# Two value banks by turns, an earlier norm of q and another order of first loads in the first phase of an attention and feed-forward kernel

## The chip, the cores and the metric

The kernel runs on one core of a Trainium2 chip. The metric is the device time of one execution in microseconds (us); for several runs the median is given. The profile names the engines PE (TensorE's matmuls), PEld (its weight loads), DVE (VectorE), ACT (ScalarE), POOL (GpSimd) and SP (SyncE, which issues most DMAs here). Each engine works through its own queue in order and waits at an instruction until what that one needs is there.

## The reference

The reference computes attention with RMS-normalized queries and keys for 8 batches, 12 heads, 448 positions and a head size of 64, and then a feed-forward block with a squared ReLU on the 3584 tokens:

```python
def rmsnorm(x, g):
    rms = np.sqrt(np.mean(x * x, axis=-1, keepdims=True) + 1e-06)
    return x / rms * g
q_n, k_n = (rmsnorm(q, g_q), rmsnorm(k, g_k))
scores = scale * np.matmul(q_n, k_n.transpose(0, 1, 3, 2))
scores = scores - np.max(scores, axis=-1, keepdims=True)
attn = np.exp(scores)
attn = attn / (np.sum(attn, axis=-1, keepdims=True) + 1e-09)
x = np.matmul(attn, v)                  # (B, H, S, D), then laid out as (B*S, H*D)
h = np.maximum(x @ w_in, 0.0)           # 768 -> 2048
out = h * h @ w_out                     # 2048 -> 768
```

All inputs and outputs are float32.

## The kernel before

**Pairs.** Two heads of one batch are worked on together as a pair, so there are 48 pairs, numbered through by batch and head. The 448 positions are three blocks of 128 and a rest of 64; the rests of an even pair and the odd pair behind it share one block. The function `alone(i)` is true for the first twelve pairs (batches 0 and 1). They are worked on with no feed-forward beside them: this is the first phase. From then on attention of later pairs is woven into the feed-forward of earlier ones.

**One pair.** The rows of q and k are squared (`square`, L179 on ACT or L181 on POOL), summed and turned into mean squares (`add`, L192 and L195 on DVE) and raised to the power -1/2 (`power`, L201 on POOL, for q and k in one instruction through its arguments `first` and `number`). Then q alone is scaled by it (`scale`, L216 on POOL); k's factor is applied later, as the scale of the exponential (L392). `turn` transposes k and q on PE (L357, L360), k into PSUM bank 7 and q into bank 6. ACT copies kT (L367), DVE copies qT and multiplies it by the gains (L365). `weigh` makes the scores into banks 0 to 3 (L387) and their exponentials on ACT (L392); as the keys lie on the partitions, this is the weight matrix already turned. `attend` multiplies the weights by the values into bank 4 (L455), `add_weights` sums them up with a matrix of ones into bank 5 (L468). `take_sums` transposes the sums by blocks on DVE (L496); `invert` makes the reciprocals in all columns (four small copies L505, then L506, L511, L512); `finish` multiplies bank 4 by them (L524) and so makes xT, the input of the feed-forward. Behind some `finish` calls `begin_forms` makes differences of xT for a fast matrix product (L548, on DVE and POOL).

**Visits.** In the first phase each pair i has two visits, n = 0 and n = 1, of `visit_alone`. Visit 0 loads v of pair i, makes two key blocks of the scores of pair i, transposes k and q of pair i+1, squares q (ACT) and k (POOL) of pair i+2, calls `begin(step)`, and attends three key blocks of pair i-1 with their first two sums. Visit 1 normalizes pair i+2 (`normalize`: both adds on DVE, one power for both, q's scaling), makes the other scores of pair i, calls `begin(step)`, issues the loads of q and k of pair i+4 and attends the last key block of pair i-1, with its last sums, `take_sums`, `invert` and `finish`. Each visit ends with `begin(step + 1)`. `step` is 4i + 2n, so four steps go to a pair.

**Weights for the feed-forward.** In between, `begin` brings the weights into another form, a piece at a time: it makes up to two pending sums of pieces (`make_sum`, L884, by turns on DVE and POOL) and, when the step has reached the next due time in the list `early`, calls `convert`. That joins the piece split before (three DVE operations, L838, L858, L862), loads the words of the piece after the next (SP, L806 or L811, three buffers) and splits one piece (three ACT operations, L825 to L827). The list `early` holds 17 times, 2.4 steps apart, beginning with step 0.

**The start.** The kernel loads the two gain rows (ACT's queue), q and k of pair 0 and of pair 1. `load_full` loads the three whole blocks of a pair's q or k with two DMAs (L157), `load_rest` the rests of two pairs with two more (L166). On ACT an exponential of one number (L83) makes it load its table; its output goes to `g_most`, which DVE overwrites with the greatest gain (L87). If that is small enough (L90, `bounded`), the program runs without a subtraction of the maximum; this is the branch that runs here. `normalize_first` prepares pairs 0 and 1, with q scaled on DVE.

**Later phases.** `visit_among` and `put_in_order` do the same work in the midst of the products, through lists of tasks. `put_in_order` calls `rescale` for a pair, hence one power and one scaling. These pairs attend into bank 4 and sum into bank 3; q's and k's transposes go through bank 0 or through DRAM. Banks 7, 6 and 5 are then the accumulators of the products (`roles`, L596).

Of the kernel before, what the change touches and what calls it, by code (L numbers as in the profile page):

```python
# [13 lines left out]
F32 = mybir.dt.float32  # L14
I32 = mybir.dt.int32
U32 = mybir.dt.uint32
AF = mybir.ActivationFunctionType
ALU = mybir.AluOpType
# [18 lines left out]
@with_exitstack  # L37
def kernel(
    ctx: ExitStack,
    tc: tile.TileContext,  # L40
    q: bass.AP,
    k: bass.AP,
    v: bass.AP,
    g_q: bass.AP,
    g_k: bass.AP,
    moe_w_in: bass.AP,
    moe_w_out: bass.AP,
    out: bass.AP,
):

    nc = tc.nc
    D = q.shape[3]
    const = ctx.enter_context(tc.tile_pool(name="const", bufs=1))
    wide = const.tile([P, P + D], F32, name="wide")
    ident = wide[:, 0:P]  # L60
    ones = const.tile([P, D], F32, name="ones")
    minus_half = const.tile([P, 1], F32, name="minus_half")
    g = const.tile([P, 1], F32, name="g")
    g_most = const.tile([1, 1], F32, name="g_most")
    bounded = const.tile([1, 1], I32, name="bounded")
    rows = Rows(nc, SimpleNamespace(io=const, small=const), q, k, ones, minus_half)
    with (
        tc.tile_pool(name="early", bufs=1) as early,
        tc.tile_pool(name="gains", bufs=1, space=bass.MemoryType.PSUM) as psum,
        tc.manual_schedule(engines=ENGINES),  # L70
    ):
        g_rows = early.tile([1, 2, D], F32, name="g_rows")
        for n, row in enumerate((g_q, g_k)):
            nc.scalar.dma_start(g_rows[:, n], row.rearrange("(one d) -> one d", one=1))
        rows.load_full(0, 0, nc.sync)
        rows.load_full(0, 1, nc.scalar)
        for x in range(2):
            rows.load_rest(0, x, nc.sync)
        for x in range(2):
            rows.load_full(1, x, nc.sync)  # L80
        nc.vector.memset(ones, 1.0)
        nc.vector.memset(minus_half, -0.5)
        nc.scalar.activation(g_most, ones[0:1, 0:1], AF.Exp)  # L83
        make_identity(nc, ident)
        nc.gpsimd.tensor_copy(out=wide[:, P : P + D], in_=ident[:, 0:D])
        nc.vector.tensor_tensor(out=g_rows[:, 0], in0=g_rows[:, 0], in1=g_rows[:, 1], op=ALU.mult)
        nc.vector.tensor_reduce(  # L87
            out=g_most, in_=g_rows[:, 0], axis=AX.X, op=ALU.max, apply_absolute_value=True
        )
        nc.vector.tensor_scalar(  # L90
            out=bounded, in0=g_most, scalar1=MOST_G, scalar2=None, op0=ALU.is_le
        )
        gains = psum.tile([P, 1], F32, name="gains")
        for e in range(2):
            nc.tensor.matmul(
                gains[ds(e * D, D), :], lhsT=g_rows[:, 0], rhs=ones[0:1, 0:1], start=True, stop=True
            )
        for x in range(2):
            rows.normalize_first(0, x, early.tile([P, 2 * P + 2 * P], F32, name=f"squares{x}"))
        nc.scalar.mul(g, gains, D**-0.5)  # L100
    flag = nc.values_load(bounded, min_val=0, max_val=1)
    with tc.If(flag > 0) as either:
        program(tc, rows, v, g, wide, moe_w_in, moe_w_out, out, shift=False)
    with either.Else():
        program(tc, rows, v, g, wide, moe_w_in, moe_w_out, out, shift=True)

class Rows:

# [1 line left out]

    def __init__(self, nc, pools, q, k, ones, minus_half):
        self.nc, self.pools, self.qk = nc, pools, (q, k)
        self.ones, self.minus_half = ones, minus_half
        self.B, self.H, self.S, self.D = q.shape
        self.rooms = [
            pools.io.tile([P, 2, NG, 2, self.D], F32, name=f"qk{n}", tag=f"qk{n}") for n in range(2)
        ]
        self.squares, self.ms, self.rr = {}, {}, {}  # L120
        self.in_blocks = lambda i: False
# [74 lines left out]
            out=ms, in0=ms, scalar1=1.0 / self.D, scalar2=1e-6, op0=ALU.mult, op1=ALU.add  # L196
        )

    def power(self, i, first, number):
        ms = self.ms[i][:, first : first + number, 0 : self.count(i)]  # L200
        self.nc.gpsimd.tensor_tensor(  # L201
            out=self.rr[i][:, first : first + number, 0 : self.count(i)], in0=ms,
            in1=self.minus_half[:, :, None].to_broadcast(list(ms.shape)), op=ALU.pow,
        )

    def normalize_first(self, i, x, room):

        self.square(i, x, room)
        self.add(i, x)
        self.power(i, x, 1)  # L210
        if x == 0:
            self.scale(i, x, self.nc.vector)

# [6 lines left out]


@with_exitstack
def program(ctx, tc, rows, v, g, wide, moe_w_in, moe_w_out, out, shift):

    nc = tc.nc

# [18 lines left out]
    dram = ctx.enter_context(tc.tile_pool(name="forms", bufs=1, space=bass.MemoryType.DRAM))  # L245

    rows = rows.go_on(io, small, lambda i: in_blocks(i))
    ones = rows.ones
    ident = wide[:, 0:P]
    lasts = [const.tile([P, 2, D], F32, name=f"lasts{n}") for n in range(2)]  # L250
    ones_of = [const.tile([P, SIDE], F32, name=f"ones_of{n}") for n in range(2)]
# [31 lines left out]
    def alone(i):  # L283

        return pairs[i][0] < 2
# [58 lines left out]
            v[b, 2 * c : 2 * c + 2, NJ * P : S].rearrange("h p d -> p h d"),  # L344
        )

    def rescale(i):
        rows.power(i, 0, 2)
        for x in range(2 if shift else 1):
            rows.scale(i, x, nc.gpsimd)  # L350

    def turn(i, x):
# [87 lines left out]
                nc.vector.tensor_copy(out=tiles[NJ][e][mine, part], in_=tr[mine, NJ, :size])  # L440

    def sums_bank(i):
        return banks[5 if alone(i) else 3][:, 0:S]

    def attend(i, some):

        order = values_of(i)  # L450
        for n in some:
            m = order[n]
            mine = ds(i % 2 * LASTS, LASTS) if m == NJ and shift else ds(0, P)
            for e in range(2):
                nc.tensor.matmul(  # L455
                    banks[4][ds(e * D, D), 0:S],
                    lhsT=lasts[i % 2][mine, e, :] if m == NJ else values[i][:, m, e, :],
                    rhs=weights[key_of(i, m), e][mine], start=n == 0, stop=n == NJ,
                )
# [60 lines left out]
    def finish(i):  # L520

        b, c = pairs[i]
        xts[b, c] = new_x()
        nc.vector.tensor_tensor(  # L524
            out=xts[b, c], in0=banks[4][:, 0:S], in1=inverse.pop(i), op=ALU.mult
        )
        for x in range(2):
            del turned[i, x]
        del values[i]
        if b == 1:  # L530
            begin_forms(c)
        elif b % 2 and c >= NK:
            complete.append((b // 2, c - NK))
# [369 lines left out]

    block, tile_pieces = COST // NBLK, 4
    ahead = 4 * tile_pieces
    early = deque(2.4 * n for n in range(ahead + 1))
    every = block / ahead
    late = deque(
        block + 2 + every * (n - 2 * tile_pieces) for n in range(len(all_pieces) - ahead)
# [44 lines left out]
    def begin(step):  # L954
        for _ in range(2):
            make_sum()
        while early and early[0] <= step:
            early.popleft()
            convert()
            end_join()  # L960
# [9 lines left out]
        if i <= last:  # L970
            rows.square(i, x, room[:, 0 : 4 * P], engine)

    def normalize(i):

        if i <= last:
            for x in range(2):
                rows.add(i, x)
            rescale(i)

    def weigh_slots(i, n):  # L980
        if not shift:
            for m in slots_of(i, n):
                weigh(i, m)
        elif n:
            weigh_shifted(i)
# [10 lines left out]
    def visit_alone(i, n):  # L996
        step = i * 2 * VISITS + 2 * n
        if n == 0:
            load_v(i)
            if i and shift:  # L1000
                attend_all(i - 1)
            weigh_slots(i, n)
            turn(i + 1, 1)
            turn(i + 1, 0)
            square(i + 2, 0, new_acc())
            square(i + 2, 1, new_acc(), nc.gpsimd)
            begin(step)
            if i and not shift:
                attend(i - 1, range(NJ))
                add_weights(i - 1, (0, 1))  # L1010
                forget(i - 1, (0, 1))
        else:
            normalize(i + 2)
            weigh_slots(i, n)
            begin(step)
            if in_blocks(i + 2):
                store_q(i + 2)
                load_blocks(i + 2, 0)
                load_blocks(i + 2, 1)
            load_qk(i + 4)  # L1020
            if i and not shift:
                attend(i - 1, (NJ,))
                add_weights(i - 1, (2, 3))
                forget(i - 1, (2, 3))
                take_sums(i - 1)
                invert(i - 1)
                finish(i - 1)
            if not alone(i) and not shift:
                additions(i)
        begin(step + 1)  # L1030

    def put_in_order(i):
        rescale(i)
        if in_blocks(i):
            steps = [lambda: store_q(i), lambda: load_blocks(i, 0)]
            for step in steps:
                tasks.extend((lambda: None, lambda: None, step))
# [100 lines left out]
```

## Time and profile before

| | |
|---|---|
| median of three runs | 1462.53 us (1461.55 to 1462.66) |
| the profiled execution | 1461.41 us |
| its span, first to last instruction | 1459.6 us |
| mean granted TensorE clock | 0.998 |
| PE busy in the first 20 us | 10.0 us |
| PE busy from 20 to 140 us | 107.4 of 120 us |
| DVE busy from 20 to 140 us | 92.4 of 120 us |
| first product of the feed-forward (L643) begins | 147.31 us |

Times inside the profile count from the span's start. A line of the timeline gives the start, the duration, the engine, the source line, the operation, what it writes and reads, how many instructions were merged, and in brackets how long the engine had been idle and what ended that. A line of the waits gives the engine and line that waited, what it waited for, the sum in us, how many times, and the longest. Matmuls are pipelined and each float32 matmul is recorded as two instructions; the duration of a merged row reaches from its first start to its last end.

### The profile page before, as it was taken

How to read it: one execution, taken by the hardware profiler on the slowest of the kernel's cores; microseconds unless marked ns; L12 is line 12 of the kernel's file. 1: busy time of each engine (PE TensorE's matmuls, PEld its weight loads, DVE VectorE, ACT ScalarE, POOL GpSimd, SP SyncE). 2: the span in 40 equal slices, each digit the busy share in tenths (PEclk: the TensorE clock that was granted, in tenths of full speed). 3: DMA queues.
4: the chain of work that ended last, by engine and by line, in shares of the span. 5: the costliest groups of instructions: out<-in, count | busy, mean ns of one | idle time of the engine just before them, and what ended most of it. 6: DMA issues, size and time to landing. Idle time of an engine off the chain costs nothing.

```text
span 1459.6 us, 15299 instructions
## 1 busy us (share of the span) xinstructions
PE 1425.6 (98%) x4932; PEld 680.2 (47%) x4932; DVE 667.3 (46%) x1269; ACT 583.7 (40%) x1102; POOL 623.2 (43%) x522
## 2 busy tenths in 40 slices
PE   6989999999999999999999999999999999999998
PEld 2323444444444444445454544445444455555554
DVE  5877356786777623324342542324334251132313
ACT  6764455747555144432514234342332403222130
POOL 4545745655555635353543545245342422021111
PEclk9999999999999999999999999999999999999999
DMA  6565336565667554444435454334523223223122
GB/s 149 164 203 137 76 85 179 168 189 165 197 175 218 160 169 103 137 113 132 118 65 165 117 183 128 109 96 99 169 64 111 82 103 135 87 76 124 38 87 79
DMA packets 309278, 188.11 MB, mean 129 GB/s; under 512 B 265796, under 2 KB 293316, under 8 KB 300996
## 3 DMA queue, kind: packets, MB, share of 16 engines
q1 hardware_dynamic: 308384, 186.84, 43.7%
q8 instruction: 41, 0.67, 0.2%
q14 instruction: 49, 0.40, 0.1%
q10 hardware_dynamic: 804, 0.20, 0.1%
HBM read 144.57 MB, written 42.40 MB: 128 GB/s over the span
## 4 chain that ended last, share of the span: by engine, by line
PE 90%; DVE 4%; issue 3%; POOL 2%; ACT 1%; DMA 1%; SPq 0%; POOLq 0%; DVEq 0%; ACTq 0%
PE bank L643 35%; PE bank L724 29%; PE bank L455 9%; PE bank L387 8%; PE bank L695 5%; PE bank L485 2%; PE bank L468 1%; POOL rr L201 1%; DMA qk<-in_q_dram 1%; DVE few L505 1%; POOL qk L216 0%; DVE inverse L512 0%; DVE out_sb L884 0%; DVE xT L524 0%; DVE acc L765 0%
## 5 line engine op out<-in xcount | busy, mean ns | idle before, releaser
L643 PE MATMUL bank<-xT,in_sb 128*128 128x448 f32 x1344 | 517.5, 542 | 0.0
L643 PEld LDWEIGHTS bank<-xT,in_sb 128*128 128x128 f32 x1344 | 251.7, 190 | 262.4 <-issue 251.1
L765 DVE TENSOR_TENSOR acc<-acc,bank 128x384 f32<-128x384 f32 x324 | 173.7, 549 | 278.8 <-PE bank L724 205.6
L392 ACT ACTIVATE wT<-bank,rr 128x448 f32<-128x448 f32 x288 | 161.1, 631 | 269.1 <-PE bank L387 249.1
L201 POOL TENSOR_TENSOR rr<-ms,minus_half 128x16 f32<-128x16 f32 (+3 forms) x50 | 125.7, 2514 | 333.1 <-DVE ms L195 299.1
L724 PE MATMUL bank<-out_sb,hid 128*128 128x384 f32 x768 | 267.6, 488 | 0.0
L663 DVE TENSOR_TENSOR hid<-bank,part 128x448 f32<-128x448 f32 x128 | 77.0, 622 | 305.3 <-PE bank L643 305.2
L724 PE MATMUL bank<-out_sb,sums 128*128 128x384 f32 x576 | 204.0, 490 | 3.1 <-DVE acc L765 3.0
L724 PEld LDWEIGHTS bank<-out_sb,hid 128*128 128x128 f32 x768 | 144.8, 190 | 107.2 <-issue 6.8
L411 POOL TENSOR_TENSOR sum<-sum,wT 128x448 f32<-128x448 f32 (+1 forms) x144 | 164.3, 1164 | 12.8 <-ACT wT L392 10.4
L387 PE MATMUL bank<-qT,kT 64*128 64x448 f32 (+1 forms) x768 | 164.0, 573 | 3.7 <-ACT qT L330 1.6
L679 POOL TENSOR_TENSOR sums<-hid 128x384 f32<-128x384 f32 x32 | 32.4, 1012 | 291.1 <-ACT hid L665 290.6
L664 ACT ACTIVATE hid<-hid 128x448 f32<-128x448 f32 x128 | 73.3, 572 | 201.0 <-DVE hid L663 200.9
L724 PEld LDWEIGHTS bank<-out_sb,sums 128*128 128x128 f32 x576 | 107.7, 190 | 87.7 <-DVE acc L765 8.2
L650 ACT COPY part<-bank 128x448 f32<-128x448 f32 x128 | 67.7, 529 | 180.5 <-PE bank L643 180.4
L455 PE MATMUL bank<-wT,vt 128*64 128x448 f32 x480 | 106.2, 546 | 0.0
L387 PEld LDWEIGHTS bank<-qT,kT 64*128 64x128 f32 (+1 forms) x768 | 55.2, 173 | 108.9 <-issue 90.8
L411 POOL TENSOR_TENSOR sum<-wT 128x448 f32<-128x448 f32 x72 | 84.1, 1188 | 45.8 <-PE bank L485 45.8
L192 DVE TENSOR_REDUCE ms<-squares 128x8 f32<-128x512 f32 (+1 forms) x68 | 41.9, 617 | 125.6 <-ACT squares L179 125.6
L695 PE MATMUL bank<-out_sb,hid 128*128 128x384 f32 x256 | 86.4, 491 | 0.0
L665 ACT ACTIVATE hid<-hid 128x448 f32<-128x448 f32 x128 | 73.8, 577 | 4.0
L695 PEld LDWEIGHTS bank<-out_sb,hid 128*128 128x128 f32 x256 | 47.6, 190 | 39.3 <-issue 5.7
(83 smaller groups left out, 1126.9 us busy)
## 6 DMA issues: line engine op xcount, KB each, us to landing
out_sb<-out_forms SPq DMA_DIRECT2D x24, 1536.0 KB, 7.4
in_sb<-in_forms SPq DMA_DIRECT2D x24, 1344.0 KB, 5.9
words<-in_moe_w_in_dram SPq DMA_DIRECT2D x32, 384.0 KB, 3.6
words<-in_moe_w_out_dram SPq DMA_DIRECT2D x32, 384.0 KB, 3.6
out_forms<-out_sb SPq DMA_DIRECT2D x8, 1536.0 KB, 6.3
in_forms<-in_sb SPq DMA_DIRECT2D x8, 1344.0 KB, 5.5
qk<-in_q_dram SPq DMA_DIRECT2D x96, 96.0 KB, 3.0
vt<-in_v_dram SPq DMA_DIRECT2D x96, 96.0 KB, 3.3
```

What stands on the lines that cost most here:

```text
L201: self.nc.gpsimd.tensor_tensor(out=self.rr[i][:, first : first + number, 0 : self.count(i)], in0=ms, in1=self.minus_half[:, :, None].to_br ...
L387: nc.tensor.matmul(sc[some], lhsT=turned[p, 1][r, keys], rhs=turned[p, 0][r, :], start=True, stop=True,)
L392: nc.scalar.activation(new_weights((i, m), e), sc, AF.Exp, scale=rows.rr[i][:, 1, 2 * m + e : 2 * m + e + 1],)
L411: nc.gpsimd.tensor_tensor(out=sums[i, e][some], in0=left[some], in1=weights[key_of(i, m), e][some], op=ALU.add)
L455: nc.tensor.matmul(banks[4][ds(e * D, D), 0:S], lhsT=lasts[i % 2][mine, e, :] if m == NJ else values[i][:, m, e, :], rhs=weights[key_of(i, ...
L643: nc.tensor.matmul(ps, lhsT=w_sb[:, IN.index(left), c, :], rhs=forms[u, c][right], start=first and c == 0, stop=c == NK - 1, skip_group_ch ...
L663: nc.vector.tensor_tensor(out=dst, in0=left, in1=right, op=op)
L664: nc.scalar.activation(dst, dst, AF.Relu)
L665: nc.scalar.activation(dst, dst, AF.Square)
L695: nc.tensor.matmul(ps, lhsT=flat[a][:, t, ds(NT * P, P)], rhs=w_sb[t][:, 2 * a + half, :], start=(a, t) == parts[0], stop=(a, t) == parts[-1],
L724: nc.tensor.matmul(ps, lhsT=lefts[left][:, t, ts(tt, P)], rhs=w_sb[t][:, OUT.index(right), :], start=first and t == 0, stop=t == 1, skip_g ...
L765: nc.vector.tensor_tensor(out=acc, in0=acc, in1=ps, op=ALU.add)
```

## The change

- The values of pair i are weighed into bank 4 or bank 5 by turns (`values_bank`), where it was always bank 4. The sums move from bank 5 to bank 6.
- `power` and `rescale` now take one of q and k. In the first phase q's add, power and scaling move from the start of visit 1 to visit 0, behind its first `begin(step)` and ahead of `attend`. k's add and power stay in visit 1, now behind the scores.
- In the later phases `put_in_order` calls the two rescalings one after the other: q's power, q's scaling, k's power.
- The due times in `early` are two steps later each.
- The first loads: q's rest goes through ACT's queue; k's full blocks go through SP's queue, ahead of k's rest.
- The exponential that loads ACT's table writes a tile of its own.
- `ones` is passed to `program` directly, without a change in what is done.

```diff
-        rows.load_full(0, 1, nc.scalar)
-        for x in range(2):
-            rows.load_rest(0, x, nc.sync)
+        rows.load_rest(0, 0, nc.scalar)
+        rows.load_full(0, 1, nc.sync)
+        rows.load_rest(0, 1, nc.sync)
...
-        nc.scalar.activation(g_most, ones[0:1, 0:1], AF.Exp)
+        nc.scalar.activation(early.tile([1, 1], F32, name="some"), ones[0:1, 0:1], AF.Exp)
...
-    def power(self, i, first, number):
-        ms = self.ms[i][:, first : first + number, 0 : self.count(i)]
+    def power(self, i, x):
+
+        ms = self.ms[i][:, x, 0 : self.count(i)]
         self.nc.gpsimd.tensor_tensor(
-            out=self.rr[i][:, first : first + number, 0 : self.count(i)], in0=ms,
-            in1=self.minus_half[:, :, None].to_broadcast(list(ms.shape)), op=ALU.pow,
+            out=self.rr[i][:, x, 0 : self.count(i)], in0=ms,
+            in1=self.minus_half.to_broadcast(list(ms.shape)), op=ALU.pow,
         )
...
-    def rescale(i):
-        rows.power(i, 0, 2)
-        for x in range(2 if shift else 1):
+    def rescale(i, x):
+        rows.power(i, x)
+        if x == 0 or shift:
             rows.scale(i, x, nc.gpsimd)
...
     def sums_bank(i):
-        return banks[5 if alone(i) else 3][:, 0:S]
+        return banks[6 if alone(i) else 3][:, 0:S]
+
+    def values_bank(i):
+        return banks[4 + i % 2 if alone(i) else 4][:, 0:S]
...
-                    banks[4][ds(e * D, D), 0:S],
+                    values_bank(i)[ds(e * D, D), :],
...
-            out=xts[b, c], in0=banks[4][:, 0:S], in1=inverse.pop(i), op=ALU.mult
+            out=xts[b, c], in0=values_bank(i), in1=inverse.pop(i), op=ALU.mult
...
-    early = deque(2.4 * n for n in range(ahead + 1))
+    early = deque(2 + 2.4 * n for n in range(ahead + 1))
...
-    def normalize(i):
+    def normalize(i, x):
 
         if i <= last:
-            for x in range(2):
-                rows.add(i, x)
-            rescale(i)
+            rows.add(i, x)
+            rescale(i, x)
...
             square(i + 2, 1, new_acc(), nc.gpsimd)
             begin(step)
+            normalize(i + 2, 0)
             if i and not shift:
                 attend(i - 1, range(NJ))
...
         else:
-            normalize(i + 2)
             weigh_slots(i, n)
+            normalize(i + 2, 1)
             begin(step)
...
     def put_in_order(i):
-        rescale(i)
+        for x in range(2):
+            rescale(i, x)
```

More of the change, by code (lines that the diff above doesn't have):

```diff
@@ L65 @@
     bounded = const.tile([1, 1], I32, name="bounded")
-    rows = Rows(nc, SimpleNamespace(io=const, small=const), q, k, ones, minus_half)
+    rows = Rows(nc, SimpleNamespace(io=const, small=const), q, k, minus_half)
     with (
@@ L102, with __init__ @@
     with tc.If(flag > 0) as either:
-        program(tc, rows, v, g, wide, moe_w_in, moe_w_out, out, shift=False)
+        program(tc, rows, v, g, wide, ones, moe_w_in, moe_w_out, out, shift=False)
     with either.Else():
-        program(tc, rows, v, g, wide, moe_w_in, moe_w_out, out, shift=True)
+        program(tc, rows, v, g, wide, ones, moe_w_in, moe_w_out, out, shift=True)
 class Rows:
-    def __init__(self, nc, pools, q, k, ones, minus_half):
+    def __init__(self, nc, pools, q, k, minus_half):
         self.nc, self.pools, self.qk = nc, pools, (q, k)
-        self.ones, self.minus_half = ones, minus_half
+        self.minus_half = minus_half
         self.B, self.H, self.S, self.D = q.shape
@@ L209, in normalize_first @@
         self.add(i, x)
-        self.power(i, x, 1)
+        self.power(i, x)
         if x == 0:
@@ L222, in program @@
 @with_exitstack
-def program(ctx, tc, rows, v, g, wide, moe_w_in, moe_w_out, out, shift):
+def program(ctx, tc, rows, v, g, wide, ones, moe_w_in, moe_w_out, out, shift):
     nc = tc.nc
@@ L247, in program @@
     rows = rows.go_on(io, small, lambda i: in_blocks(i))
-    ones = rows.ones
     ident = wide[:, 0:P]
```

## The prediction

> **What bounds the kernel now.** I read the page's busy shares first, then TensorE's waits in the first 160 us, then the first phase instruction by instruction. PE is busy for 98% of the span. Behind 160 us its waits come to 4.6 us in all (3.0 and 1.6), so nothing that this change does to DVE or POOL there can bring much. The first phase is different:
>
> ```profile
> PE 1425.6 (98%) x4932; PEld 680.2 (47%) x4932; DVE 667.3 (46%) x1269; ACT 583.7 (40%) x1102; POOL 623.2 (43%) x522
> ...
> PE bank L455 <- DVE xT L524: 8.7, 7, 3.2
> PE bank L357 <- POOL qk L216: 3.5, 5, 1.0
> ```
>
> L455 is the weighing of values, and it waits seven times for `finish` (L524) to empty bank 4. L357 is q's transposition, waiting five times for POOL's scaling. In the timeline the worst case reads:
>
> ```profile
> 72.05 2.85 DVE L505 COPY few<-inverse 32x14 f32<-32x14 f32 x4
> 72.09 0.83 POOL L216 TENSOR_TENSOR qk<-qk,rr 128x384 f32<-128x384 f32 x1
> ...
> 72.88 0.99 POOL L884 TENSOR_TENSOR in_sb<-in_sb 128x384 f32<-128x384 f32 x1
> ...
> 73.84 1.03 POOL L181 TENSOR_TENSOR acc<-qk 128x512 f32<-128x512 f32 x1
> ...
> 76.10 0.62 DVE L524 TENSOR_TENSOR xT<-bank,inverse 128x448 f32<-128x448 f32 x1
> 76.64 0.67 DVE L365 TENSOR_SCALAR qT<-bank,g 128x448 f32<-128x448 f32 x1
> ...
> 76.78 1.12 PE L455 MATMUL bank<-wT,lasts 128*64 128x448 f32 x4 [3.15 <-DVE xT L524]
> ...
> 77.69 1.71 PE L455 MATMUL bank<-part,vt 128*64 128x448 f32 x4
> ```
>
> The four copies of `invert` stretch from 0.7 to 2.85 us behind three POOL operations, xT is late, PE idles 3.15 us and then runs at half pace (four matmuls 1.71 us; 0.92 elsewhere).
>
> **The size of the prize.** The first L455 of each pair's visit starts at 23.72, 33.96, 44.37, 54.38, 64.78, 76.78, 88.89, 98.38, 109.31, 119.95, 130.83 and 140.36. Less the waits inside, a cycle is 8.83 us where the visit is an odd pair's and 9.75 where it is an even one's. Six and five of these are 101.7; the trace took 116.6. So 14.9 us can go at most: 8.7 at L455, 3.5 at L357, 1.6 of slow clock behind 76.78 (twelve matmuls in 4.04 instead of 2.41 us), and some 1.1 in transposes that lost their overlap.
>
> **Part by part.**
>
> *Two value banks.* L455 no longer waits for the previous pair's xT but for the one before, a whole cycle old. Taken alone: 8.7 + 1.6 us. The clock gate needs weighing here. The Trainium skill ("TensorE: Matmul & The Clock Gate", Part 1) puts the half clock behind an idle window of about 3.4 us; by that, 3.15 us would not trigger it and 1.6 would not be mine to claim. The row shows doubled durations and the granted clock of 76.78 to 88.89 is 0.86, so the trace decides and I count 1.6.
>
> *The sums move to bank 6, which q's transposes use (L354).* This is the added wait. `add_weights` of n = 0 now follows DVE's qT copy (L365), which was read by nobody for several us; all of PE's queue stands behind it. Let S be the end of a visit's last L468. PE reaches the next sums at S + 5.2 (scores 1.71, two transposes 1.1, attend 2.41, as rows at 105.33 to 111.7 without their wait). DVE runs L496 to L524 in 3.2 us from S + 0.1, then the conversion or sum of `begin(step+1)`, then qT 0.7. Without a conversion qT ends at S + 4.0: free, slack 1.2. With one (0.36 + 0.56 + 0.56) it ends at S + 5.5: 0.3 us of wait. Behind pair 6 the subtraction of L548 adds 0.65.
>
> *Conversions two steps later.* They now fall on steps 2, 5, 7, 10, 12, 14, 17, 19 and so on to 41. Those between xT and qT (step = 3 mod 4) are 7, 19, 31; before they were 3, 15, 27, 39. Waits: 0.3 + 0.3 + 0.95 (31 has L548 too) = 1.6 us. Each conversion also issues a load of words on SP (L806, L811) that waits until DVE's L862 has freed its buffer (up to 5.5 us), and the loads of v and of q and k stand behind it. The tightest is v's last rows behind a conversion of step 3 mod 4: issued by S + 7, landed 3.2 later at S + 10, wanted at S + 12. So SP's queue costs nothing.
>
> *q's norm half a visit sooner.* In n = 0, DVE's add (0.68 + 0.17) stands behind qT and ends near S + 5; POOL's power and scaling end by S + 8, or S + 9.5 with a conversion ahead. PE wants q about S + 11 (one cycle and 2.2 more, the scores and k's transposes). The 3.5 us go with 1.5 us to spare. POOL's order becomes square k, power q, scale q, power k. Behind DVE's add stands nothing that PE needs before the next L496; ACT's square of q is done by then (65.50, qT 65.51).
>
> *A power of its own.* One 128x16 power takes 2.92 us, a 128x8 one 1.65; a 128x12 one 2.34, a 128x6 one 1.32. That is +0.38 or +0.30 us a pair on POOL, some 4 us in this phase and 11 later, on an engine at 43% and beside PE: nothing. Later phases even get q 1.3 us sooner.
>
> Here the skill speaks against the change: "SBUF — State Buffer" (Who interferes with whom) says DVE operations that use both ports and GpSimd lock each other out for the whole instruction. By that rule any power would hold up `few` or a conversion, and two of them would cost up to 3.3 us a pair, 36 us in all. The rows differ:
>
> ```profile
> 93.97 2.50 POOL L201 TENSOR_TENSOR rr<-ms,minus_half 128x12 f32<-128x12 f32 x1 [7.64 <-DVE ms L195]
> ...
> 95.09 0.65 DVE L496 STREAM_TRANSPOSE inverse<-bank 128x448 f32<-128x448 f32 x1 [0.74 <-PE bank L468]
> ...
> 95.78 0.72 DVE L505 COPY few<-inverse 32x14 f32<-32x14 f32 x4
> ```
>
> Under a power the copies take 0.72; only squares, scalings and sums block. By the row the powers cost nothing, but they sheltered the copies: of the twelve `few` groups eight took 0.7 to 0.8, five of them beside a power, which kept POOL's other work away. In the new order a square of k (1.04) may land there. Below: none does (0). Above: each visit pays what 72.05 paid, 2.15 us. I take the present average: excess 4.1 at L505 and some 5.7 on L838, L858, L884 and L195, so 0.9 a visit; half of the eleven visits are tight (a conversion, a sum or lateness of DVE up to 1 us ahead of qT) with 0.3 left: 6 x 0.6 = 3.6 us.
>
> *The first loads.* q's rest is issued by ACT at 1.56 and 2.27 in place of SP at 1.76 and 2.47; it lands last (5.30) and the squares start then: 0.3 us. k's full rows move to SP, ending near 2.7 as before (2.85); k's rest and pair 1 come 0.4 us sooner, so nothing is pushed behind. *The separate Exp target* frees L87 from the table load (4.37), but q's chain (squares 5.40, power 7.04, L216 8.73, transposed at 9.48) doesn't pass through it; only k's transposes at 7.03 may come sooner, and they are 2 us early: nothing.
>
> *No conversion in visit 0.* Its three ACT operations (17.12 to 18.69) stood ahead of the exps; L387 at 19.27 waited 0.82 and took 2.59 for what elsewhere takes 1.77: 1.6 us. q of pair 2 was 0.7 late at 23.13 and now just in time. With 0.3 this is 2.6; I take 2.2, since power q stands behind the square of k.
>
> **Sum.** 14.9 - 1.6 - 3.6 + 2.2 = 11.9, call it 12 us: 1449.4 against the profiled run's 1461.41 (span 1459.6). The runs' median is 1.1 higher, so 1450.5. The later phases keep PE full and pass the gain on: the last conversion at step 41 and its sums (44) are done eight steps before the first product.
>
> **Rivals.**
> - *Everything hides* (12%): the new bank wait never bites. 14.9 + 2.2 = 17 us, 1445.5. For: the mean DVE load, 8.0 us a visit, is below PE's 9.25. Against: four of the pairs' cycles have 9.4 to 11.3.
> - *DVE becomes the bound* (19%): conversions pile up in front of L496 and qT, costing another 4 to 8 us; 1454 to 1458, say 1456. For: DVE at 87% from 40 to 80 us, and pace rises by a tenth.
> - *Slower through bank 6* (4%): qT late in every visit, with blocked copies (2.15) and on average 1.3 us of conversion ahead: 3.3 + 2.15 + 1.3 + 0.7 - 5.2 = 2.25 a visit, 25 us against 17: 1470. It decides from 1.55 us a visit. Against: only the copies at 72.05 and 116.17 show this.
> - *It does nothing* (3%): another semaphore keeps L455 waiting; 1462. The waits name xT, so hardly.
>
> **The numbers.** My case (62%) spans gains of 8 to 15. With the first rival whole and the near half of the second the range is 1445.5 to 1457.5. About 0.2% (2.9 us) can be told from no change. Faster: 62 + 12 + 17 = 91%; same: the tail of DVE's case and the do-nothing, 5%; slower 4%.
>
> **What would show it.** Right: "L455 <- xT" and "L357 <- qk" gone from PE's waits before 160 us; L468 waiting for qT three to six times, under 1 us each; first product (L643) at 135 instead of 147; granted clock 1.00 from 60 to 100 us. Wrong: L468 waiting over 1.5 us a visit, `few` above 2 us in most visits, a late L496, or a gain at 147 that is gone by the end.

## The result, and the profile after

| | before | after |
|---|---|---|
| median of four runs | 1462.60 us (1461.55 to 1463.02) | 1453.39 us (1452.14 to 1454.01) |
| ratio, 95% interval | | 0.9937 (0.992 to 0.9954) |
| span of the profiled execution | 1459.6 us | 1451.4 us |
| first weighing of values begins | 23.72 us | 21.75 us |
| first product begins (L643, now L646) | 147.31 us | 140.75 us |
| from there to the end | 1312.3 us | 1310.65 us |
| DVE busy from 20 to 140 us | 92.4 us | 101.7 us |

The change gains 9.2 us by the medians and 8.2 us by the two spans; 1450.5 us was forecast. The rows below the span split the 8.2 us: 2.0 at the start, 4.6 in the steady part of the first phase (123.6 us before, 119.0 after), 1.6 behind the first product.

The source lines have moved: L201 is now L202 and L216 L217, and below the new function lines stand three further down (L455 is L458, L468 L471, L496 L499, L505 L508, L524 L527, L548 L551, L884 L887). First the busy shares and TensorE's waits of the kernel after, up to 160 us and, in the last line, behind (sum in us, times, longest):

```profile
PE 1422.7 (98%) x4932; PEld 680.3 (47%) x4932; DVE 673.8 (46%) x1269; ACT 584.9 (40%) x1102; POOL 644.1 (44%) x568
...
PE bank L471 <- DVE qT L365: 7.5, 5, 1.8
...
PE bank L458 <- DMA lasts<-in_v_dram: 1.6, 1, 1.6
...
PE bank L357 <- issue: 0.5, 1, 0.5
PE bank L357 <- POOL qk L217: 0.5, 1, 0.5
...
PE bank L727 <- DVE acc L768: 3.3, 4, 1.3
```

Behind 160 us the kernel before had these two:

```profile
PE bank L724 <- DVE acc L765: 3.0, 4, 1.3
PE bank L387 <- ACT qT L330: 1.6, 3, 0.7
```

The waits for xT are gone and those for q's scaling have shrunk from 3.5 us to 0.5. In their place stand the sums (L471), waiting five times for the qT copy that empties bank 6. This is the added wait that was forecast, but 7.5 us in all where 1.6 + 3.6 were counted, and 1.05 to 1.81 us each where under 1 was expected. The one "issue" wait is bank 6 again, by its time: the transposes at 50.39 start when `take_sums` (L499, 49.65 to 50.29) has read the bank. Two changes had no place in the forecast: v's last rows came too late once, and behind 160 us the three waits of L387 for q (1.6 us) are missing.

The longest of the five, in the timeline of the kernel after:

```profile
88.99 0.65 DVE L499 STREAM_TRANSPOSE inverse<-bank 128x448 f32<-128x448 f32 x1 [0.82 <-PE bank L471]
...
89.54 1.04 POOL L181 TENSOR_TENSOR acc<-qk 128x512 f32<-128x512 f32 x1
89.68 1.48 DVE L508 COPY few<-inverse 32x14 f32<-32x14 f32 x4
...
93.01 0.62 DVE L551 TENSOR_TENSOR xT<-xT 128x448 f32<-128x448 f32 x1
...
93.55 0.35 DVE L841 TENSOR_SCALAR out_sb<-words 128x384 uint32<-128x384 uint32 x1
93.94 0.56 DVE L861 SCALAR_TENSOR_TENSOR out_sb<-words,out_sb 128x384 uint32<-128x384 uint32 x1
94.64 0.56 DVE L865 CUSTOM_DVE_ANT_0 out_sb<-words,out_sb 128x768 uint16<-128x768 uint16 x1
95.11 0.68 DVE L365 TENSOR_SCALAR qT<-bank,g 128x448 f32<-128x448 f32 x1
...
95.84 0.57 PE L471 MATMUL bank<-wT,ones_of 128*32 128x448 f32 x2 [1.81 <-DVE qT L365]
```

This is the visit that was forecast as the worst (step 31): the subtraction L551 and a conversion (L841 to L865) stand ahead of qT. The forecast had 0.95 us for that and 0.6 for a blocked copy. The copies L508 took 1.48 us in place of 0.7, beside POOL's square of k; 0.95 and this excess of 0.78 make up nearly the whole 1.81 us.

v's last rows, in the rows of POOL, of SP's queue and of PE:

```profile
99.52 1.04 POOL L217 TENSOR_TENSOR qk<-qk,rr 128x512 f32<-128x512 f32 x1
100.52 1.32 POOL L887 TENSOR_TENSOR out_sb<-out_sb 128x384 f32<-128x384 f32 x1
...
101.87 0.34 SPq L889 DMA_DIRECT2D out_forms<-out_sb  x1
...
109.91 1.23 SPq L337 DMA_DIRECT2D vt<-in_v_dram  x2
111.18 0.62 SPq L342 DMA_DIRECT2D lasts<-in_v_dram  x1
...
113.55 0.97 PE L458 MATMUL bank<-wT,lasts 128*64 128x448 f32 x4 [1.56 <-DMA lasts<-in_v_dram]
```

SP issues a finished piece's store (L889) only when POOL has summed it up (L887). That sum's input had been ready at 97.95, but POOL first ran a power and q's scaling for the pair ahead. Behind the store wait a load of words, the loads of q and k (until 109.8), and then v: a delay on POOL that has passed through SP's queue to PE.

### The profile page after: what moved, and what is told of

Read it like the earlier page. It is cut to its first block, busy times and chain, and to the rows that moved or that the text cites. A ratio compares the mean times of both kernels' runs of the same rounds, so it can differ in the third digit from the quotient of the medians.

```text
span 1451.4 us, 15319 instructions
## 1 busy us (share of the span) xinstructions
PE 1422.7 (98%) x4932; PEld 680.3 (47%) x4932; DVE 673.8 (46%) x1269; ACT 584.9 (40%) x1102; POOL 644.1 (44%) x568
## 4 chain that ended last, share of the span: by engine, by line
PE 93%; DVE 4%; issue 1%; ACT 1%; DMA 1%; POOL 0%; SPq 0%; ACTq 0%; DVEq 0%; POOLq 0%
PE bank L646 35%; PE bank L727 30%; PE bank L387 9%; PE bank L458 9%; PE bank L698 5%; PE bank L488 2%; PE bank L471 1%; DVE few L508 1%; DVE in_sb L865 0%; DVE out_sb L887 0%; DVE inverse L515 0%; DVE in_sb L861 0%; DVE in_sb L841 0%; PE bank L357 0%; DVE qT L365 0%
## 5 line engine op out<-in xcount | busy, mean ns | idle before, releaser
L646 PE MATMUL bank<-xT,in_sb 128*128 128x448 f32 x1344 | 517.5, 542 | 0.0
L646 PEld LDWEIGHTS bank<-xT,in_sb 128*128 128x128 f32 x1344 | 251.7, 190 | 262.4 <-issue 249.4
L202 POOL TENSOR_TENSOR rr<-ms,minus_half 128x8 f32<-128x8 f32 (+1 forms) x96 | 146.4, 1525 | 249.7 <-DVE ms L195 238.8
L411 POOL TENSOR_TENSOR sum<-sum,wT 128x448 f32<-128x448 f32 (+1 forms) x144 | 163.6, 1159 | 16.2 <-ACT wT L392 13.8
L387 PE MATMUL bank<-qT,kT 64*128 64x448 f32 (+1 forms) x768 | 163.6, 573 | 1.4 <-DVE qT L365 1.1
L458 PE MATMUL bank<-wT,vt 128*64 128x448 f32 x480 | 106.2, 546 | 0.0
L387 PEld LDWEIGHTS bank<-qT,kT 64*128 64x128 f32 (+1 forms) x768 | 55.2, 173 | 106.3 <-issue 86.9
```

Source lines behind the costliest of these rows:

```text
L202: self.nc.gpsimd.tensor_tensor(out=self.rr[i][:, x, 0 : self.count(i)], in0=ms, in1=self.minus_half.to_broadcast(list(ms.shape)), op=ALU.pow,)
L387: nc.tensor.matmul(sc[some], lhsT=turned[p, 1][r, keys], rhs=turned[p, 0][r, :], start=True, stop=True,)
L411: nc.gpsimd.tensor_tensor(out=sums[i, e][some], in0=left[some], in1=weights[key_of(i, m), e][some], op=ALU.add)
L458: nc.tensor.matmul(values_bank(i)[ds(e * D, D), :], lhsT=lasts[i % 2][mine, e, :] if m == NJ else values[i][:, m, e, :], rhs=weights[key_o ...
L646: nc.tensor.matmul(ps, lhsT=w_sb[:, IN.index(left), c, :], rhs=forms[u, c][right], start=first and c == 0, stop=c == NK - 1, skip_group_ch ...
```

## The experiments

Each kernel ran in three rounds beside the kernel before; ratios are to it, with 95% intervals. "FP" is the start of the first product, "FW" that of the first weighing of values. Letters in an expectation stand for the theory and its rival as they are worded there. The theory going in: the bank waits and q's waits cover each other, so each part alone uncovers the other's wait; what remains after both is DVE late with qT, through POOL's work. The rival: the parts simply add up, and the remainder has another cause. The kernel before itself took 1462.60 us beside the kernel after and 1461.20 to 1461.65 beside these, so between runs the ratios compare better than the medians. In norm_only and banks_norm some lines stand one further (L456, L525; L366, L388, L472).

**One part of the change at a time.** On the kernel before: only the banks, only the norm, only the start (first loads, Exp target and due times), in this order.

```diff
-        return banks[5 if alone(i) else 3][:, 0:S]
+        return banks[6 if alone(i) else 3][:, 0:S]
+
+    def values_bank(i):
+        return banks[4 + i % 2 if alone(i) else 4][:, 0:S]
...
```

```diff
...
             begin(step)
+            normalize(i + 2, 0)
...
-            normalize(i + 2)
             weigh_slots(i, n)
+            normalize(i + 2, 1)
...
     def put_in_order(i):
-        rescale(i)
+        for x in range(2):
+            rescale(i, x)
```

```diff
-        rows.load_full(0, 1, nc.scalar)
-        for x in range(2):
-            rows.load_rest(0, x, nc.sync)
+        rows.load_rest(0, 0, nc.scalar)
+        rows.load_full(0, 1, nc.sync)
+        rows.load_rest(0, 1, nc.sync)
...
-        nc.scalar.activation(g_most, ones[0:1, 0:1], AF.Exp)
+        nc.scalar.activation(early.tile([1, 1], F32, name="some"), ones[0:1, 0:1], AF.Exp)
...
-    early = deque(2.4 * n for n in range(ahead + 1))
+    early = deque(2 + 2.4 * n for n in range(ahead + 1))
```

> The kernel before with the two value banks and the sums in bank 6 alone. Theory A (the waits are coupled through DVE: whatever is freed on one side is partly paid on the next): the 8.7 us of L455 waiting for xT go, but q's transposes now wait longer for POOL's scaling (3.5 us before, 6 to 8 now) and the sums wait for the qT copy some 3 us; the first product starts 4 to 5 us sooner than 147.3, the span is 1454 to 1456. Theory B (the parts are independent and add up): the slow clock and the 8.7 us go whole, first product at 137 to 139, span 1449 to 1451.

> The kernel before with q's norm in visit 0 and a power for each of q and k alone, in the first phase and in the later ones. Theory A: the 3.5 us of L357 waiting for the scaling go, but L455 then waits for xT in their place (11 to 13 us where it was 8.7), so that the first product starts at most 2 us sooner (145.5 to 147.3); behind it the 1.6 us go in which L387 waited for qT of L330, so the span is 1456 to 1458. Theory B: 3.5 us go in the first phase, first product at 143 to 144, span 1454 to 1455. Theory C (POOL's moved work blocks DVE's copies more than before): first product later than 147.3.

> The kernel before with the order of the first loads, the separate target of the first exponential and the conversions two steps later, nothing else. Theory A: the first weighing of values starts at 21.8 to 22.5 instead of 23.7 (2 us come from the loads and the missing conversion in visit 0, not from q's norm); 1 to 2 us of it are left at the first product, span 1457.5 to 1458.5. Theory B (q's scaling of pair 2 is what frees the start): it starts at 23 or later, and the span is within 1 us of 1459.6.

| | median us | ratio | span | FP |
|---|---|---|---|---|
| banks_only | 1459.89 | 0.9985 (0.9978 to 0.9992) | 1456.5 | 144.5 |
| norm_only | 1458.28 | 0.998 (0.9971 to 0.9988) | 1457.1 | 145.8 |
| start_only | 1465.34 | 1.0031 (1.0019 to 1.0044) | 1463.1 | 150.7 |

TensorE's waits up to 160 us, of the three in turn:

```profile
PE bank L357 <- POOL qk L216: 6.0, 9, 2.1
PE bank L471 <- DVE qT L365: 4.3, 3, 2.2
```

```profile
PE bank L456 <- DVE xT L525: 13.8, 11, 2.0
```

```profile
PE bank L455 <- DVE xT L524: 12.6, 8, 3.0
PE bank L357 <- POOL qk L216: 5.3, 4, 2.1
```

With only the banks, most of the 8.7 us at the values turn into other waits: for q 6.0 us in place of 3.5, and at the sums 4.3. With only the norm, q is in time, and PE arrives at bank 4 earlier and waits there eleven times, 13.8 us. Each part alone uncovers the other's wait. The start alone makes the kernel slower, which neither theory had. In its timeline of PE and POOL:

```profile
21.28 1.04 POOL L216 TENSOR_TENSOR qk<-qk,rr 128x512 f32<-128x512 f32 x1
...
22.38 0.55 PE L357 MATMUL bank<-wide,qk 128*128 128x128 f32 x3 [2.11 <-POOL qk L216]
```

PE runs through the first scores without the conversion's delay and has transposed k by 20.3, but then waits 2.11 us for q, which still comes late without the early norm. The weighing begins at 22.96, 0.76 us sooner than before, but the steady part then takes 4.2 us longer: L455 waits 12.6 us in place of 8.7, once 2.98 us with slow matmuls behind. Which of the moved conversions causes this was not tried.

**The two parts together, and the due times by themselves.** `banks_norm` is the kernel before with both (or the kernel after without first loads, Exp target and due times); `old_due_times` is the kernel after with `early` from step 0, so the two differ in the first loads and the Exp target alone.

```diff
-    early = deque(2 + 2.4 * n for n in range(ahead + 1))
+    early = deque(2.4 * n for n in range(ahead + 1))
```

> The kernel before with the two value banks, the sums in bank 6 and q's early norm, but with the old first loads and the old due times. Theory A (banks and norm each only uncover the other's wait when alone): together they take more than the 3.1 and 2.5 us of span that they took alone: first product at 140.5 to 142.5, span 1451 to 1453. Theory B (they add up): first product at 143, span 1454.

> The kernel after with the conversions due from step 0 again. Theory A (the later due times matter only through the conversion in visit 0 and through which visits have a conversion between xT and the qT copy): the first weighing of values starts at 22.8 to 23.5 instead of 21.75; the waits of L471 for qT stay at 6 to 9 us; first product at 141.5 to 143.5 instead of 140.7, span 1452 to 1454. Theory B (later due times are a loss by themselves, as the 3.5 us lost with the first loads alone suggest): first product before 140, span under 1450.5.

| | median us | ratio | span | FW | FP |
|---|---|---|---|---|---|
| banks_norm | 1450.66 | 0.9924 (0.9908 to 0.9941) | 1449.5 | 22.52 | 138.61 |
| old_due_times | 1450.67 | 0.9925 (0.9908 to 0.9941) | 1448.8 | 22.63 | 138.69 |

The waits up to 160 us of banks_norm and of old_due_times:

```profile
PE bank L472 <- DVE qT L366: 5.2, 6, 1.3
...
PE bank L388 <- ACT wT L393: 1.3, 1, 1.3
```

```profile
PE bank L471 <- DVE qT L365: 5.2, 6, 1.3
...
PE bank L357 <- issue: 1.1, 2, 0.6
...
PE bank L357 <- POOL qk L217: 0.8, 1, 0.8
PE bank L387 <- ACT wT L392: 0.4, 1, 0.4
```

Alone the two parts took 3.1 and 2.5 us off the span; together they take 10.1, more than the change as a whole. First loads and Exp target can't be seen: 1450.66 against 1450.67. The later due times are a loss, as the rival in the expectation of old_due_times had it: 2.1 us at the first product and 2.6 in the span. By the ratios (0.9925 against 0.9937) it is some 1.7 us, with intervals that overlap. They do what they were forecast to do at the start: the wait of the scores for ACT (1.3 and 0.4 us in these two) is gone in the kernel after, where FW is 0.9 sooner. But from there to the first product both kernels with the old times take 116.1 us and the kernel after takes 119.0: the sums wait 7.5 us in place of 5.2 and v's last rows 1.6, while the transposes wait 1.0 in place of 1.9.

**Where the waits at the sums come from.** Two ways to cut them: sums in bank 7, which k's transposes use (the products' bank list turned round to match), or POOL's square of k given to ACT, which leaves the bank as it is and frees DVE's copies.

```diff
-        return banks[6 if alone(i) else 3][:, 0:S]
+        return banks[7 if alone(i) else 3][:, 0:S]
...
-    roles = [banks[n] for n in (7, 6, 5)]
+    roles = [banks[n] for n in (6, 7, 5)]
```

```diff
-            square(i + 2, 1, new_acc(), nc.gpsimd)
+            square(i + 2, 1, new_acc())
```

> The kernel after, with the sums in bank 7 (k's transposes, copied by ACT) instead of bank 6 (q's, copied by DVE); the first two product banks are exchanged so that the first product doesn't wait for the last sums. Theory A (the 7.5 us in which L471 waits for the qT copy come from the shared bank): these waits go; scores of even pairs wait for qT at most 2 us in all, k's copy on ACT costs under 1 us; first product 4 to 6 us sooner (135 to 137), span 1445.5 to 1447.5. Theory B (DVE's load is the bound and the waits only move): the scores or the transposes wait instead, first product less than 2 us sooner, span 1449.5 or more.

> The kernel after, with k's squares in the first phase on ACT instead of POOL. Theory A (the copies L508 are held up by POOL's square of k, and this makes the qT copy late): the four copies take 0.7 to 0.9 us in at least ten of twelve groups (their excess is 5.0 us in all in the kernel after), L471 waits 3 to 5 us for qT instead of 7.5, first product at 137 to 139, span 1447.5 to 1449.5. Theory B (it is DVE's amount of work or its order, not the blocking): L471 waits 6.5 us or more and the first product stays within 1 us of 140.7. Theory C: ACT becomes late (it gets 0.6 us a pair more, 0.53 to 0.63 each) and the scores wait for its exponentials; first product later than 141.

> The same with the conversions due from step 0, where the run old_due_times had 1450.67 and a first product at 138.7. Theory A (the later due times cost 2.7 us because they put more of POOL's work beside DVE's path to qT): without the square beside it the two sets of due times come within 1.2 us of each other (before: 2.1 at the first product). Theory B (the later due times cost by themselves): the difference of 2 us or more stays.

> The sums in bank 7 as in the run sums_in_7, with the conversions due from step 0. Theory A: without the wait for the qT copy the due times matter by the start alone: first weighing of values 1 to 1.7 us later than 21.6, first product 135.5 to 137, span 1446.3 to 1447.8; the 1.3 us of waiting for v's last rows may go with the other places of the stores. Theory B (DVE is the bound by now): first product within 0.4 us of 135.0 or sooner.

| | median us | ratio | span | FP |
|---|---|---|---|---|
| sums_in_7 | 1446.85 | 0.9899 (0.9883 to 0.9916) | 1445.8 | 134.97 |
| sums_7_old_due | 1446.42 | 0.9897 (0.988 to 0.9913) | 1444.8 | 134.72 |
| k_squares_act | 1448.51 | 0.9909 (0.9892 to 0.9925) | 1446.5 | 135.90 |
| k_squares_act_old_due | 1449.82 | 0.9918 (0.9902 to 0.9935) | 1447.4 | 136.67 |

The waits of sums_in_7 and of k_squares_act up to 160 us:

```profile
PE bank L357 <- DVE inverse L499: 3.4, 4, 1.3
...
PE bank L458 <- DMA lasts<-in_v_dram: 1.3, 1, 1.3
```

```profile
PE bank L471 <- DVE qT L365: 3.8, 5, 1.0
...
PE bank L458 <- DMA lasts<-in_v_dram: 1.6, 1, 1.6
```

In bank 7 the sums wait for nothing, since ACT takes kT out of that bank early (at 92.03 in the kernel after, where qT is at 95.11); k's transposes wait instead for L499 to read the sums, 3.4 us in all. DVE's instructions are the same as in the kernel after, so their amount was not the bound.

With the squares on ACT the copies of `few` take 0.70 to 0.86 us in eleven of twelve visits (after: five of twelve), the waits at the sums halve, and FP comes 4.85 us sooner, more than expected (137 to 139). The five waits can be compared one by one, in us:

| the wait of L471 at (kernel after) | 34.17 | 55.17 | 65.97 | 95.84 | 127.44 |
|---|---|---|---|---|---|
| kernel after | 1.18 | 1.75 | 1.05 | 1.81 | 1.73 |
| k_squares_act | 0.44 | 0.96 | 0.43 | 1.05 | 0.94 |
| the wait is shorter by | 0.74 | 0.79 | 0.62 | 0.76 | 0.79 |
| L508 ahead of it is shorter by (second: L509) | 0.74 | 0.79 | 0.62 | 0.78 | 0.80 |

The first column, in the timelines of the kernel after and of k_squares_act:

```profile
28.64 1.50 DVE L508 COPY few<-inverse 32x14 f32<-32x14 f32 x4
28.66 1.05 POOL L181 TENSOR_TENSOR acc<-qk 128x512 f32<-128x512 f32 x1
...
34.17 0.57 PE L471 MATMUL bank<-wT,ones_of 128*32 128x448 f32 x2 [1.18 <-DVE qT L365]
```

```profile
28.16 0.76 DVE L508 COPY few<-inverse 32x14 f32<-32x14 f32 x4
...
32.95 0.57 PE L471 MATMUL bank<-wT,ones_of 128*32 128x448 f32 x2 [0.44 <-DVE qT L365]
```

What the stretched copies lose comes back at the sums to within 0.02 us. The last pair of runs bears on the due times: with the squares off POOL the later times no longer cost anything (1448.51 against 1449.82), and in bank 7 they make 0.4 us. In these runs their loss shows only with the squares on POOL and the sums in a bank that waits for qT. In bank 7 the first product was expected at 135.5 to 137 with the old times; it came at 134.72, as the rival had it.

**The gain behind the first product.** The kernel after with one power for q and k in `put_in_order`, as before; nothing of the first phase differs.

```diff
     def put_in_order(i):
-        for x in range(2):
-            rescale(i, x)
+        ms = rows.ms[i][:, :, 0 : rows.count(i)]
+        nc.gpsimd.tensor_tensor(
+            out=rows.rr[i][:, :, 0 : rows.count(i)], in0=ms,
+            in1=rows.minus_half[:, :, None].to_broadcast(list(ms.shape)), op=ALU.pow,
+        )
+        for x in range(2 if shift else 1):
+            rows.scale(i, x, nc.gpsimd)
```

> The kernel after, but in the later phases with one power for q and k ahead of q's scaling, as before. Theory A (what is gained behind the first product comes from q being ready some 1.3 us sooner there): first product at 140.7 as in the kernel after, the 1.6 us in which L387 waited for the qT of L330 are back, span 1452.5 to 1453.5. Theory B (that gain is only another alignment of the streams): no such waits, span 1451 to 1452.

1455.55 us, ratio 0.9957 (0.9941 to 0.9974). From the first product to the end 1312.0 us: 1312.3 before, 1310.65 after. Its waits behind 160 us:

```profile
PE bank L727 <- DVE acc L768: 3.0, 4, 1.3
PE bank L387 <- ACT qT L330: 1.6, 3, 0.7
```

The second line is back, as before the change. The stretch from the first product to the end is 1312.0 to 1312.4 us in all four kernels with one power there (before, banks_only, start_only and this one) and 1309.6 to 1311.3 in the ten with separate powers.

Its FP (141.58) is also 0.8 us later than the kernel after's, in a first phase that is the same program. Its weighing starts sooner (20.98), and its waits at the sums, of the transposes and for v's rows also come to 10.1 us, but divided otherwise: the sums wait 8.8 us, and v's last rows, issued at 110.87, only 0.2, since PE comes later. The rest is a slow clock:

```profile
94.97 0.57 PE L471 MATMUL bank<-wT,ones_of 128*32 128x448 f32 x2 [1.82 <-DVE qT L365]
...
95.86 3.23 PE L387 MATMUL bank<-qT,kT 64*128 64x448 f32 x12
```

The scores took 3.23 us where the kernel after, behind the same wait of 1.81, took 1.94. The granted clock from 96 to 100 us was 0.57 here and 1.00 there.

**v's last rows.** Their load is issued ahead of v's two others in `load_v`, on top of sums_7_old_due; then with the squares of k on ACT as well.

```diff
+        mine = ds(i % 2 * D, D)
+        nc.sync.dma_start(
+            lasts[i % 2][mine],
+            v[b, 2 * c : 2 * c + 2, NJ * P : S].rearrange("h p d -> p h d"),
+        )
         for e in range(2):
             nc.sync.dma_start(
...
-        mine = ds(i % 2 * D, D)
-        nc.sync.dma_start(
-            lasts[i % 2][mine],
...
```

> The run sums_7_old_due with v's last rows issued ahead of its other rows. Theory A (the 1.8 us in which L458 waits for v's last rows come from SP's queue: a store that waits for POOL's sum, four loads of q and k and two of v stand ahead): the last rows are issued 1.2 us sooner, the wait falls to 0.6 or less, first product 133.4 to 134.2, span 1443.5 to 1444.3. Theory B (they wait for their place, which the products of an earlier pair still read): no change, 134.7 and 1444.8.

> The run sums_7_lasts_first with k's squares on ACT as well. Theory A: the transposes' 2.0 us of waiting for the sums' transposition L499 shrink to under 1, first product 132.5 to 133.5, span 1442.5 to 1443.5, the best of all. Theory B (with the sums in bank 7 there is slack enough, and ACT pays): within 0.6 us of sums_7_lasts_first, or slower.

The first took 1447.02 us, ratio 0.99 (0.9883 to 0.9916), FP 134.63 against 134.72: no gain, though the wait that it aimed at fell from 1.80 to 0.26 us, as theory A had it. The timeline shows why:

```profile
126.52 0.97 PE L458 MATMUL bank<-wT,lasts 128*64 128x448 f32 x4 [0.26 <-DMA lasts<-in_v_dram]
127.37 1.66 PE L458 MATMUL bank<-part,vt 128*64 128x448 f32 x3
128.44 0.59 PE L458 MATMUL bank<-acc,vt 128*64 128x448 f32 x1
128.86 0.54 PE L458 MATMUL bank<-part,vt 128*64 128x448 f32 x1
```

Now v's full blocks (vt) come last. Three matmul instructions are spread over 1.66 us and the fourth starts at 128.86, a delay that is not listed as a wait. It belongs to the whole queue, so an order within the queue moves it and doesn't remove it. The second took 1445.18 us (1444.83 to 1446.25), ratio 0.9889 (0.9872 to 0.9905), FP 133.71. The time is about as expected; the transposes still wait 1.6 us for L499 where under 1 was expected. It has the lowest ratio of all: 16.5 us below the kernel before, where the change gains 9.2.

## Why the forecast was right, and where its steps were not

The sum was 14.9 us of stalls, less 1.6 and 3.6 that come back, plus 2.2 at the start: 11.9. The spans give 8.2. Of the signs that were named for the case, these came: the waits for xT gone, the waits for q's scaling nearly so, five waits at the sums, and a granted clock of 1.00 from 60 to 100 us. Two did not: each of the five is over 1 us, and the first product begins at 140.75 in place of 135. The median gain, 9.2, lies at the low end of the 8 to 15 that the case spanned.

- **Two value banks; q's norm.** Right: "L455 <- xT" is gone and "L357 <- qk" went from 3.5 to 0.5 us. That the stalls go only when both parts are there is shown by the two runs with one each.
- **The wait through bank 6, conversions.** Right: steps 7, 19 and 31 were named, and the sums wait at 34.17, 65.97 and 95.84, each time behind a conversion ahead of qT. The forecast had 0.3, 0.3 and 0.95 us for these visits without a blocked copy; k_squares_act, where the copies there are not blocked, has 0.44, 0.43 and 1.05.
- **The wait through bank 6, blocked copies.** The mechanism is right and the size is not: 3.6 us were counted, on the present average of POOL's work, and 7.5 - 1.6 = 5.9 were waited; a late release of the bank cost the transposes another 0.5. "A square of k may land there": four of the groups of `few` stretch beside a square (28.64, 39.59, 60.56 and 89.68), and the first, third and fourth add 0.7 to 0.8 us each to the three waits above. The one at 39.59 costs nothing, with no conversion ahead of qT. Two more waits come in visits without a conversion between xT and qT. At 55.17 (1.75) a conversion ahead of L499, itself stretched by POOL's sum, had made L499 2 us late, the second rival's mechanism; then `few` (1.59) and L509 (0.96) were stretched as well. At 127.44 (1.73) `few` and a sum on DVE took 1.52 and 1.48 us, beside POOL's sum and its part of L551.
- **Due times.** Wrong. "Conversions two steps later" was costed at 1.6 us in the steady part, by where conversions fall, and at a gain of 1.6 at the start. Old times had their own conversions between xT and qT (3, 15, 27, 39), so the 1.6 is no difference between the two. Measured, the later times lose 2.9 us between the first weighing and the first product and gain 0.9 at the start. They bring more of the copies beside POOL's other work: six groups of `few` take over 1.25 us, four of them beside a square; with the old times it is four, two of them beside a square.
- **"So SP's queue costs nothing".** Wrong by 1.6 us in this trace; in one_power_later, where PE came later, by 0.2. The working followed SP from a load of words behind DVE's L862; it left out the stores, which wait on SP for POOL's sums, and the sum here stood behind q's power and scaling on POOL.
- **The start.** 2.2 us forecast, 2.0 measured, but not by the parts that were named: the banks and the norm alone bring FW to 22.52, hence 1.2. The due times add some 0.9. The first loads' 0.3 can't be seen.
- **Later phases.** The forecast said that they "get q 1.3 us sooner" and valued it at nothing. It was worth the three waits of L387 for qT, 1.6 us. They stood among the 4.6 us of waits behind 160 us; the step that failed was to put these aside as too small to matter, without asking what released them.
- **Powers.** That two powers cost nothing fits what is seen: POOL is busy 644.1 us in place of 623.2 (some 15 were counted, 20.9 came), no wait of PE names a power, and `few` takes 0.72 us wholly beside one (131.89). The 36 us of the shared-port rule did not come.

So the misses in the spans were 4.9 us too little waiting in the first phase (10.1 us in place of 5.2: 7.5 at the sums, 0.5 + 0.5 of the transposes, 1.6 for v's rows) and 1.6 too little gain behind it. The medians, which stood 1.1 us above the profiled execution before and stand level with it (1453.40) after, gave another one back. That these partly cancel, so that the median is missed by 2.9 us only, is luck. Open: what the first loads are worth by themselves was not tried, only as a difference of two kernels, and a gain or loss below 1 us at the start can't be told from the 0.8 us between two traces of the same phase.

## What to carry to other kernels

When two waits take turns on one engine, taking away either gives little and taking away both gives more than their sum: work out the cycle with all of them gone and with each one left. When a buffer is moved to a place that another engine empties, list everything that can stand ahead of that emptying in its engine's order, and everything that can stretch it, for each visit and not on the average. And follow a queue of DMAs back to what its stores wait for: a store behind a slow sum holds up every load behind it.

## What the runs showed of the hardware

- POOL's powers leave DVE's copies alone, its squares, scalings and sums don't. In the kernel after, `few` at 131.89 took 0.72 us wholly beside a power. The group at 89.68 lay 0.9 us beside a square of k and took 1.48; the one at 121.38 lay 0.94 us beside a sum and took 1.52; in old_due_times the one at 49.16 lay 0.84 us beside a scaling and took 1.30. The excess over 0.7 is a little less than the overlap. The Trainium skill ("SBUF — State Buffer", Who interferes with whom) has the lock with DVE's two-port instructions for GpSimd as a whole; by these rows not every operation of it counts. Whether that lies in the operation or in its size is not shown: a power here has 6 or 8 columns, the others 384 or 512.
- PE's clock fell behind idle stretches of very different length. In start_only four matmul instructions took 1.70 us in place of 0.92 behind 2.98 us (at 56.11), with a granted clock of 0.50 from 56 to 62 us. It fell behind 2.23 us in banks_only (119.54; 0.58 and 0.57 in the next two stretches of 2 us) and behind 1.82 in one_power_later (94.97; 0.57 from 96 to 100). Behind 1.81 us in the kernel after (95.84) and 2.17 in start_only (134.34) it stayed at 1.00. So the length of the idle stretch alone does not decide it in these traces, and the 3.4 us weighed in the forecast is no safe limit. What decides it stays open.
- Two traces of the same first phase differed by 0.8 us at the first product and at the first weighing (20.98 and 21.75 us), as much as some of the terms of the sum.
